# A four-layer attention kernel: gates folded into the memory's mask and into ScalarE's copy, residual sums of layer B moved from VectorE to ScalarE and GpSimd

## The chip, the cores and the metric

The kernel runs on one core of one Trainium2 chip, as one launch. The metric is device time in microseconds (us) for the whole program. TensorE (PE) does the matrix products, with its weight loads shown apart (PEld), VectorE (DVE) and ScalarE (ACT) the work on tiles, GpSimd (POOL) some of the elementwise work, and SyncE (SP), ScalarE and GpSimd issue the transfers.

## The reference

Four layers in the order A, B, A, B, each a residual sum on a layer norm; sequence S = 2048, width D = 640, H = 32 heads of 20. Layer A is linear attention, layer B causal attention within 4 segments of 512 rows plus a memory of the earlier segments. The part of B that the change touches:

```python
g = sigmoid(beta)                       # one gate per head
for s in range(4):
    logits = einsum(qs, ks) * scale + mask
    p = softmax(logits)
    a_dot = einsum(p, vs)
    pq = phi(qs)                        # phi(t) = t + 1 if t > 0 else exp(t)
    a_mem = einsum(pq, M) / (einsum(pq, z) + 1e-6)
    outs.append(g * a_mem + (1.0 - g) * a_dot)
    M = M + einsum(phi(ks), vs);  z = z + sum(phi(ks))
x = x + concat(outs) @ wo               # the residual sum
```

## The kernel before

**The streams.** PE's instructions stand in an order that the program writes (MANUAL names PE alone). Kernel.run mixes two generators by the costs that each reports: dense (projections, layer norms, memory, output projections) and attention. The order of DVE, ACT, POOL and SP, and which of the 8 banks of PSUM each product is written to, are left to the scheduler. A bank (tag "ps") is handed on when the last reader of the product in it is done, so a matrix product of one stream can wait for a reader of the other.

**Attention of layer B.** A segment has 8 groups of 4 heads, so each layer has 32 groups and the program 64. The table STRETCHES lists a group's steps in three stretches; a slot works on three groups at once: row maxima of the newest, exponentials of the one before, and the sums and the output of the oldest. In a slot:

- row_max (L687, L694): PE multiplies queries by keys into two banks, DVE takes the row maximum of each piece with a custom instruction on 128, 256, 384 or 512 columns, each followed by a short read of the accumulator into mg.
- split_max and max_rows (L703 to L718): the maxima are split into two fp16 numbers, turned by PE and copied into two spare rows of the query stack, so that a second product subtracts them.
- scores (L729, L733, L740): PE writes the shifted scores, ACT takes exponentials (pe, ten buffers), POOL zeroes what lies above the diagonal.
- weigh (L756): PE multiplies the exponentials by the values; the values carry a 21st column of ones per head, so that row 20 of a head's 32 rows is the softmax denominator.
- evacuate (L762): ACT copies the 128x512 result from PSUM to oTf.
- normalize (L769 to L782): PE turns oTf in four pieces into one bank; DVE takes the reciprocal of the denominators (L772, 128x16), multiplies it by 1 - g (L773, 128x16), and multiplies the values by it (L781, or L778 in segment 0), which is the last reader of the bank; POOL adds the product to what the memory gave (L782).

Just after the four turns PE issues the first maxima's products and the second group's first scores, so DVE's queue there holds, beside L772, L773 and L781, the two 512-wide row maxima of the newest group.

**Memory of layer B.** phi of the keys times the values is added up in acc (L587, L589). masked (L478) multiplies acc by the block mask blk, which keeps each head to its own rows. read_mem (L359) multiplies phi of the queries by that; DVE adds 1e-6 to the denominators (L377), takes the reciprocal (L378), for layer B multiplies by the gate (L380), and multiplies the values (L381). Layer B calls it for the four row tiles of each of segments 1 to 3, two halves each, 48 halves in the two layers.

**Output of layer B.** b_out turns the rows of a segment (turn, L268 to L273), multiplies them by wo in two halves of 320 columns (proj_n, 15 products each), and o_half (L391) takes each half from PSUM with one DVE instruction: times a scale, plus the rows of x. When both halves are done, ACT's queue issues the transfer of the row tile (L662). Each layer B has 16 row tiles, so 32 halves, 64 in the program. In the first layer B these lie between 560 and 1022 us, mixed with layer A; in the last one all four segments' outputs stand behind the projections, in the last 150 us, beside the last nine groups' attention.

**Queues.** Loads and q, k stores go by SP, the fetches of weights and phi of layer A's queries by POOL, the row tiles x by ACT.

## Time and profile before

| what | value |
|---|---|
| median of 3 runs | 1830.17 us (1827.09 to 1830.6) |
| profiled execution: time, span | 1833.06 us, 1831.3 us |
| mean granted TensorE clock | 0.995 |
| PE busy | 1713.7 us, 94% of the span, 13032 instructions |
| DVE busy | 1145.0 us, 63%, 3890 instructions |
| ACT busy | 911.1 us, 50%, 1696 instructions |
| POOL busy | 502.5 us, 27%, 925 instructions |
| opening, 0 to 130 us: PE busy | 111.23 us |
| 130 to 310 us, first half of layer A: PE busy | 179.75 of 180 us |
| 310 to 998 us, attention of the first layer B: PE busy | 635.99 of 688 us |
| 998 to 1220 us, second layer A: PE busy | 221.71 of 222 us |
| 1220 to 1831.3 us, attention of the last layer B: PE busy | 565.01 of 611.3 us |

Shares are of the span, the time from the first to the last instruction on the core; the profiled execution took 1.8 us more than its span. The clock is the share of full speed that TensorE was granted. A line like L694 is a line of the kernel before; the changed kernel's lines are some 13 to 15 higher from L391 on (L694 is its L708, L733 its L747, L762 its L776, L772 its L786, L781 its L793, L662 its L676, L272 its L284).

In a row of the timeline stand the start in us, the duration in us, the engine, the line, the operation, the tiles (written <- read), the shape, and in brackets how long the engine had been idle before it and what ended that. "mg" in such a bracket is the end of a row maximum: PE waited for the bank that the maximum had read.

### The profile page before, as it was taken

The numbers are of one execution on the slowest core, as the hardware profiler recorded it, in microseconds if no ns is written. First come the engines' busy times: TensorE is split into PE (matmuls) and PEld (weight loads), VectorE is DVE, ScalarE is ACT, GpSimd is POOL, SyncE is SP. The second block draws the span as 40 slices with busy tenths as digits, with TensorE's granted clock in tenths as the row PEclk, the third lists the DMA queues.
The fourth block names the chain that finished last, engine by engine and source line by source line (L and its number), as shares of the span: only waits on it lengthen the run. The fifth ranks groups of instructions, "written<-read, shape, count | busy, mean of one in ns | idle before, by whom it ended". The sixth has DMA issues, their size and how long they took to land.

```text
span 1831.3 us, 36161 instructions
## 1 busy us (share of the span) xinstructions
PE 1713.7 (94%) x13032; PEld 1070.3 (58%) x13032; DVE 1145.0 (63%) x3890; ACT 911.1 (50%) x1696; POOL 502.5 (27%) x925
## 2 busy tenths in 40 slices
PE   6999999999999999898989999999999989998998
PEld 4666676654664565453556776766546546544555
DVE  7655343677777676766663421527687777777783
ACT  5455433256556545545554433333664665565553
POOL 1534440022122113224344334200221231232231
PEclk9999999999999999999999999999999999999999
DMA  7452443312222332352212112432122222323332
GB/s 254 154 188 92 159 143 99 107 58 93 88 67 86 105 103 76 105 186 71 66 56 87 51 33 91 137 108 99 51 91 92 86 90 91 101 77 100 122 112 87
DMA packets 123307, 185.96 MB, mean 102 GB/s; under 512 B 13676, under 2 KB 85484, under 8 KB 120952
## 3 DMA queue, kind: packets, MB, share of 16 engines
q1 hardware_dynamic: 109416, 137.44, 23.5%
q0 software_dynamic: 4496, 25.23, 3.8%
q10 hardware_dynamic: 9216, 20.98, 3.0%
q8 instruction: 103, 1.69, 0.4%
q14 instruction: 76, 0.62, 0.1%
HBM read 104.41 MB, written 78.64 MB: 100 GB/s over the span
## 4 chain that ended last, share of the span: by engine, by line
PE 75%; DVE 11%; ACT 6%; issue 4%; POOL 2%; DMA 2%; SPq 1%; POOLq 0%; ACTq 0%; DVEq 0%
PE ps L325 33%; PE ps L311 18%; PE ps L756 7%; DVE junk L694 4%; PE ps L268 4%; ACT pe L733 3%; PE ps L370 3%; PE ps L729 3%; PE ps L452 2%; PE ps L687 2%; POOL e L341 1%; PE ps L582 1%; PE ps L769 1%; DVE nat L547 1%; PE ps L574 1%
## 5 line engine op out<-in xcount | busy, mean ns | idle before, releaser
L694 DVE CUSTOM_DVE_ANT_0 junk<-ps,maskw 128x512 bf16<-128x512 f32 (+3 forms) x1024 | 499.5, 488 | 83.2 <-PE ps L687 27.1
L733 ACT ACTIVATE pe<-ps,lsc 128x512 f32<-128x512 f32 x640 | 392.7, 691 | 174.5 <-PE ps L729 171.5
L740 POOL TENSOR_SCALAR_AFFINE_SELECT pe<-pe 128x256 f32<-128x256 f32 (+1 forms) x640 | 233.5, 371 | 677.4 <-ACT pe L733 672.0
L325 PEld LDWEIGHTS <-xT 128*128 128x128 f16 x2880 | 281.7, 99 | 124.1 <-issue 18.6
L325 PEld LDWEIGHTS <-oT 128*128 128x128 f16 x1920 | 187.1, 98 | 79.6 <-issue 7.6
L341 POOL TENSOR_SCALAR e<-e 128x320 f32<-128x320 f32 (+1 forms) x104 | 163.7, 1574 | 163.2 <-ACT e L337 154.4
L756 PE MATMUL ps<-pe,v 128*32 128x512 f32 (+3 forms) x2048 | 155.4, 438 | 13.7 <-ACT pe L733 6.8
L729 PE MATMUL ps<-qs,ks 62*128 62x384 f16 (+3 forms) x1024 | 132.2, 299 | 33.4 <-DVE mg L694 22.4
L325 PE MATMUL ps<-w_Bo,oT 128*128 128x320 f16 x960 | 142.8, 301 | 2.6 <-DVE mg L694 1.4
L325 PE MATMUL ps<-w_Bv,xT 128*128 128x320 f16 x960 | 141.3, 301 | 1.9 <-DVE mg L694 1.9
L325 PE MATMUL ps<-w_Av,xT 128*128 128x320 f16 x960 | 141.2, 305 | 1.6 <-DVE w_Av L234 1.0
L311 PE MATMUL ps<-xT,w_Bq 128*128 128x512 f16 x600 | 139.5, 379 | 1.5 <-DVE mg L694 0.9
L311 PE MATMUL ps<-xT,w_Bk 128*128 128x512 f16 x600 | 139.5, 379 | 0.2 <-DVE xn L391 0.2
L325 PE MATMUL ps<-w_Ao,oT 128*128 128x320 f16 x960 | 139.5, 299 | 0.0
L311 PE MATMUL ps<-xT,w_Aq 128*128 128x512 f16 x600 | 136.0, 379 | 1.3 <-DVE xT L273 0.9
L325 PE MATMUL ps<-w_Ak,xT 128*128 128x320 f16 x960 | 135.6, 299 | 1.4 <-DVE mg L694 1.4
L348 ACT ACTIVATE v<-ps 128x320 f32<-128x320 f32 x128 | 55.4, 436 | 143.2 <-PE ps L325 138.9
L291 POOL TENSOR_TENSOR rs<-rs,mhalf 128x1 f32<-128x1 f32 x64 | 35.3, 551 | 302.6 <-DVE rs L290 302.6
L687 PE MATMUL ps<-ks,qs 60*128 60x512 f16 (+3 forms) x1024 | 108.4, 297 | 5.8 <-ACT pe L733 3.6
L756 PEld LDWEIGHTS ps<-pe,v 128*32 128x32 f32 x2048 | 65.3, 110 | 81.2 <-issue 66.3
L547 DVE SCALAR_TENSOR_TENSOR nat<-ps,nat 128x512 f16<-128x512 f32 x80 | 55.3, 691 | 90.3 <-ACT nat L546 86.4
L546 ACT ACTIVATE nat<-ps 128x512 f16<-128x512 f32 x80 | 48.0, 600 | 105.9 <-PE ps L311 76.3
(151 smaller groups left out, 2240.9 us busy)
## 6 DMA issues: line engine op xcount, KB each, us to landing
x<-xn ACTq DMA_DIRECT2D x48, 320.0 KB
qs<-qd SPq DMA_DIRECT2D x128, 120.0 KB
ks<-kd SPq DMA_DIRECT2D x128, 120.0 KB
xo<-x SPq DMA_DIRECT2D x48, 320.0 KB
pqd<-pq POOLq DMA_DIRECT2D x40, 256.0 KB, 2.5
pqi<-pqd SPq DMA_DIRECT2D x32, 320.0 KB
qd<-nat SPq DMA_DIRECT2D x40, 256.0 KB
kd<-nat SPq DMA_DIRECT2D x40, 256.0 KB
```

The costliest lines, as they stand in the source:

```text
L268: nc.tensor.transpose(pt[:, (c - c0) * P:(c - c0 + 1) * P], src[:, c * P:(c + 1) * P], self.ident)
L311: nc.tensor.matmul(p, w[:, c, a, t * P:(t + 1) * P], xT[:, c, b, :], start=k == 0, stop=k == 3 * C - 1)
L325: nc.tensor.matmul(p, xT[:, c, a, i * P:(i + 1) * P], w[:, c, b, n * HN:(n + 1) * HN], start=k == 0, stop=k == 3 * C - 1)
L341: nc.gpsimd.tensor_scalar(e, e, 1.0, eps, op0=OP.min, op1=OP.add)
L348: self.nc.scalar.activation(vv[:, n * HB:(n + 1) * HB, :DH], p.rearrange("p (h e) -> p h e", e=DH), AF.Copy, scale=V_SHIFT)
L547: nc.vector.scalar_tensor_tensor(nat[:, 1], p, QK_SHIFT, nat[:, 0], op0=OP.mult, op1=OP.subtract)
L687: nc.tensor.matmul(bs[par][:, a:a + n], qs[r, p, i * P:(i + 1) * P], ks[r, p, :n], start=True, stop=True)
L694: nc.vector.tensor_tensor_reduce(junk[:, :n], bs[par][:, a:a + n], self.maskw[:, SEG - n:], 1.0, NEG, OP.add, OP.max, G["mg"][:, par, p, i ...
L729: nc.tensor.matmul(b[:, a:a + n], ks[r, p, j * P:(j + 1) * P], qs[r, p, j * P:], start=True, stop=True)
L733: nc.scalar.activation(e, b, AF.Exp, scale=self.lsc)
L740: nc.gpsimd.affine_select(d, d, pattern=pat, compare_op=OP.is_ge, fill=0.0, base=0, channel_multiplier=-1)
L756: nc.tensor.matmul(G["pv"][32 * h4:32 * h4 + 32, j * P:], v[j][:, h * E1:h * E1 + 32], G.pop((p, par, j)), start=j == 0, stop=j == 2, skip ...
```

## The change

Three edits, and a smaller ring for POOL's transfers.

1. **1 - g** moves into evacuate. A new tile cg (128 x 8) holds 1/(1 - g) in the four rows where the denominators of a group's heads lie, 1 elsewhere. It is filled once by four small transfers on SP, one exponential on ACT, and a memset and a two-step tensor_scalar on DVE. The copy of L762 multiplies by a column of it, so the denominators arrive multiplied by 1/(1 - g) and the reciprocal of L772 brings 1 - g with it. L773 is gone (64 instructions).
2. **g** moves into the mask. gblk is blk with its value columns multiplied by the gate, made once by a 128x756 copy and five tensor_tensor on DVE; masked takes it for layer B. L380 is gone (48 instructions).
3. **The residual sum** of layer B's output, for all but the last segment of the last layer B (56 of 64 halves): instead of one DVE instruction, ACT copies the half from PSUM with the scale (new L404) and POOL adds the rows of x in place (new L405). The transfer L662 (new L676), on ACT's queue, now follows POOL's add.

The ring that POOL's transfers use shrinks from 8192 to 4096 bytes.

```diff
     def gates(self):
...
+        self.cg = cp.tile([P, NG], F32, name="cg")
+        nc.vector.memset(self.cg, -1e4)
+        for h4 in range(4):
+            nc.sync.dma_start(self.cg[32 * h4 + DH:32 * h4 + DH + 1],
+                              bass.AP(tensor=beta.tensor, offset=beta.offset + h4, ap=[[0, 1], [4, NG]]))
         nc.scalar.activation(g, g, AF.Exp, scale=-1.0)
+        nc.scalar.activation(self.cg, self.cg, AF.Exp)
         nc.vector.tensor_scalar(g, g, 1.0, None, op0=OP.add)
         nc.vector.reciprocal(g, g)
-        self.gate = g
-        self.gate1 = cp.tile([P, H], F32, name="gate1")
-        nc.vector.tensor_scalar(self.gate1, g, -1.0, 1.0, op0=OP.mult, op1=OP.add)
+        nc.vector.tensor_scalar(self.cg, self.cg, 1.0, 2.0 ** 100, op0=OP.add, op1=OP.min)
+        self.gblk = cp.tile([P, MW], F32, name="gblk")
+        nc.vector.tensor_copy(self.gblk, self.blk)
+        for t in range(C):
+            n = HI[t] - LO[t] + 1
+            b = self.gblk[:, OFF[t]:OFF[t] + WID[t]].rearrange("p (h e) -> p h e", e=E1)[:, :, :DH]
+            nc.vector.tensor_tensor(b, b, g[:, LO[t]:HI[t] + 1, None].to_broadcast([P, n, DH]), op=OP.mult)
...
-    def read_mem(self, pq, mem, dst, mul=None):
+    def read_mem(self, pq, mem, dst):
...
-            if mul is not None:
-                nc.vector.tensor_tensor(rc, rc, mul[:, k * HB:(k + 1) * HB], op=OP.mult)
...
-    def o_half(self, oT, wo, L, x, xn, n):
+    def o_half(self, oT, wo, L, x, xn, n, later=False):
+        nc = self.nc
         p = self.proj_n(oT, wo, 0, n)
-        self.nc.vector.scalar_tensor_tensor(xn[:, n * HN:(n + 1) * HN], p, self.io[L],
-                                            x[:, n * HN:(n + 1) * HN], op0=OP.mult, op1=OP.add)
+        c = slice(n * HN, (n + 1) * HN)
+        if later:
+            nc.scalar.activation(xn[:, c], p, AF.Copy, scale=self.io[L])
+            nc.gpsimd.tensor_tensor(xn[:, c], xn[:, c], x[:, c], op=OP.add)
+        else:
+            nc.vector.scalar_tensor_tensor(xn[:, c], p, self.io[L], x[:, c], op0=OP.mult, op1=OP.add)
...
-                st["mem"] = self.masked(acc)
+                st["mem"] = self.masked(acc, self.gblk)
...
-                self.o_half(oT[i], wo, "B", x, xn, n)
+                self.o_half(oT[i], wo, "B", x, xn, n, later=not st.get("ends"))
...
-        self.nc.scalar.activation(G["oT"], G["pv"], AF.Copy)
+        self.nc.scalar.activation(G["oT"], G["pv"], AF.Copy, scale=self.cg[:, G["g"]:G["g"] + 1])
...
-        nc.vector.tensor_tensor(rc, rc, self.gate1[:, None, 4 * g:4 * g + 4].to_broadcast([P, NT, 4]),
-                                op=OP.mult)
...
+                segs[-1]["ends"] = True
```

PE's instructions keep their order in the whole program; 1915 of its 2372 products go to another bank than before, since the banks follow their readers. DVE, ACT and POOL are ordered anew by the scheduler. Two places show how.

The first is DVE in the group of the last layer B that is normalized at 1741 us (the fourth of the last nine). Before, the reciprocal is followed by the two 512-wide maxima with L773 between them, and only then by the product L781, which reads the bank of the turned output:

```order
3585 L273 TENSOR_TENSOR oT<-ps,oT 128x2x128
3586 L391 SCALAR_TENSOR_TENSOR xn<-ps,ioB,xo 128x320
3587 L772 RECIPROCAL rc_22429<-ps 128x16
3588 L694 ISA junk,mg<-ps,maskw 128x512
3589 L694 ISA mg 128x1
3590 L773 TENSOR_TENSOR rc_22429<-rc_22429,gate_2322 128x16
3591 L694 ISA junk,mg<-ps,maskw 128x512
3592 L694 ISA mg 128x1
3593 L781 TENSOR_TENSOR tmp<-ps,rc_22429 128x320
3594 L694 ISA junk,mg<-ps,maskw 128x384
```

The same place in the changed kernel:

```order
3443 L285 TENSOR_TENSOR oT<-ps,oT 128x2x128
3444 L786 RECIPROCAL rc_22378<-ps 128x16
3445 L708 ISA junk,mg<-ps,maskw 128x512
3446 L708 ISA mg 128x1
3447 L793 TENSOR_TENSOR tmp<-ps,rc_22378 128x320
3448 L708 ISA junk,mg<-ps,maskw 128x512
3449 L708 ISA mg 128x1
3450 L708 ISA junk,mg<-ps,maskw 128x384
```

The residual sum (L391) and L773 are gone, and the product (L781, now L793) stands between the two maxima instead of behind both. PE's third product after the two is then written to the product's bank instead of the second maximum's. The same exchange is found in most of the 64 groups: the sequence reciprocal, maximum, L773, maximum, product, with nothing else between, stands in 36 groups before; reciprocal, maximum, product in 40 after.

The second is ACT in the same group. Before, the copy of the group's result is followed by a piece of the turned rows, the transfer of the row tile, and four exponentials:

```order
1193 L762 ACTIVATE oTf<-ps 128x512
1194 L272 ACTIVATE oT<-ps 128x2x128
1195 L662 DMA out_x<-xn 128x640
1196 L733 ACTIVATE pe<-ps,lsc 128x512 x4
1197 L272 ACTIVATE oT<-ps 128x3x128
```

And after:

```order
1245 L776 ACTIVATE oTf<-ps,cg 128x512
1246 L284 ACTIVATE oT<-ps 128x2x128
1247 L404 ACTIVATE xn<-ps,ioB 128x320
1248 L676 DMA out_x<-xn 128x640
1249 L747 ACTIVATE pe<-ps,lsc 128x512 x4
1250 L284 ACTIVATE oT<-ps 128x3x128
1251 L404 ACTIVATE xn<-ps,ioB 128x320
```

The scaled copy stands ahead of the transfer, and the transfer, which reads what POOL adds to that copy, ahead of the exponentials. The copy, the transfer and exponentials stand directly behind one another like this at 5 places of the program, 4 of them in the last 150 us; at the other row tiles the transfer stands later in ACT's queue.

More of the change, by code (lines that the diff above doesn't have):

```diff
@@ L462, in memory @@
             if s == NSEG - 1:
-                L["mem"] = self.masked(acc)
+                L["mem"] = self.masked(acc, self.blk)
         if behind:
@@ L474, in a_first, with masked @@
             yield from queries(range(2, C))
-    def masked(self, acc):
+    def masked(self, acc, blk):
         mem = self.sb.tile([P, MW], F32, tag="mem", name="mem", bufs=2)
-        self.nc.vector.tensor_tensor(mem, acc, self.blk, op=OP.mult)
+        self.nc.vector.tensor_tensor(mem, acc, blk, op=OP.mult)
         return mem
@@ L626, in b_memory @@
             for i in range(NT):
-                yield from self.read_mem([q[:, i * P:(i + 1) * P] for q in st["pq"]], mem,
-                                         st["o"][:, i], self.gate)
+                yield from self.read_mem([q[:, i * P:(i + 1) * P] for q in st["pq"]], mem, st["o"][:, i])
         st["remembered"] = True
@@ L1010 @@
     arrays["const"] = constants()
-    nc = bacc.Bacc("TRN2", target_bir_lowering=False, num_devices=1, dynamic_dma_scratch_size=8192)
+    nc = bacc.Bacc("TRN2", target_bir_lowering=False, num_devices=1, dynamic_dma_scratch_size=4096)
     build(nc, arrays)
```

## The prediction

> **What bounds the kernel now.** I read the chain of waits first. By engine it says:
>
> ```profile
> PE 75%; DVE 11%; ACT 6%; issue 4%; POOL 2%; DMA 2%; SPq 1%; POOLq 0%; ACTq 0%; DVEq 0%
> ```
>
> TensorE sets the end. Nothing in the change removes work of PE, so it can only shorten PE's idle time. The second view, the windows of the two attention stretches, says how much there is (columns: length, then busy time of PE, PEld, DVE, ACT, POOL):
>
> ```profile
> 310.00:998.00 688.00, 635.99 (x5015) 380.01 (x5013) 467.39 (x1700) 363.54 (x673) 181.98 (x393) 1.00 0.28 91
> 1220.00:1831.30 611.30, 565.01 (x4586) 334.81 (x4584) 442.27 (x1629) 328.24 (x606) 142.79 (x356) 0.99 0.29 94
> ```
>
> PE is idle 688.00 - 635.99 = 52.0 us in the first and 611.30 - 565.01 = 46.3 us in the second: 98.3 us is the most that can be won. DVE is busy 909.7 us of these 1299.3 and ACT 691.8, neither full. The third view, PE's waits, says whom PE waits for (us in total, times, longest):
>
> ```profile
> PE ps L729 <- DVE mg L694: 22.4, 42, 1.0
> PE ps L268 <- DMA x<-in_A_x: 11.5, 1, 11.5
> PE ps L268 <- DVE mg L694: 7.1, 15, 0.5
> PE ps L756 <- ACT pe L733: 6.8, 17, 0.7
> PE pm L712 <- DVE m L704: 6.0, 9, 1.2
> PE ps L325 <- DVE mg L694: 5.2, 10, 1.0
> ...
> PE ps L370 <- DVE rc L377: 3.2, 4, 0.8
> ```
>
> The largest item by far is the end of a row maximum on DVE: 22.4 + 7.1 + 5.2 = 34.7 us in 67 waits, a third of the idle time. The change touches the place where these waits arise. The fourth view is DVE's timeline in one group, normalized at 1741 us:
>
> ```profile
> 1740.75 0.55 DVE L391 SCALAR_TENSOR_TENSOR xn<-ps,ioB,xo 128x320 f32<-128x320 f32 x1 [0.99 <-PE ps L325]
> 1741.22 0.25 DVE L772 RECIPROCAL rc<-ps 128x16 f32<-128x16 f32 x1
> 1741.51 0.69 DVE L694 CUSTOM_DVE_ANT_0 junk<-ps,maskw 128x512 bf16<-128x512 f32 x1
> 1742.12 0.08 DVE L694 DVE_READ_ACCUMULATOR2_ANT mg<- 128x1 f32 x1
> 1742.12 0.17 DVE L773 TENSOR_TENSOR rc<-rc,gate 128x16 f32<-128x16 f32 x1
> 1742.35 0.69 DVE L694 CUSTOM_DVE_ANT_0 junk<-ps,maskw 128x512 bf16<-128x512 f32 x1
> 1742.97 0.08 DVE L694 DVE_READ_ACCUMULATOR2_ANT mg<- 128x1 f32 x1
> 1742.97 0.48 DVE L781 TENSOR_TENSOR tmp<-ps,rc 128x320 f32<-128x320 f32 x1
> 1743.37 0.55 DVE L694 CUSTOM_DVE_ANT_0 junk<-ps,maskw 128x384 bf16<-128x384 f32 x1
> ```
>
> and PE's next step there:
>
> ```profile
> 1743.10 0.55 PE L268 MATMUL ps<-ident,ol 128*128 128x128 f32 x3 [0.47 <-DVE mg L694]
> ```
>
> The second 512-wide maximum starts at 1742.35 and takes 0.69, so it ends at 1743.04; PE starts at 1743.10, 0.06 later, in the bank that this maximum had read. It had waited 0.47.
>
> This recurs all over both stretches. I sorted PE's waits behind the two 512-wide maxima of a group into three kinds: 26 single waits of 0.47 behind the second (390.38 below is the first, 1743.10 above one of the last), ten pairs of 0.35 behind the first and 0.47 behind the second (432.10 with 432.94 is the first), and 18 single waits of 0.3 to 1.05 behind the first only, where DVE had other work ahead of it (1683.11 is the last):
>
> ```profile
> 390.38 0.44 PE L268 MATMUL ps<-ident,xh 128*128 128x128 f32 x2 [0.47 <-DVE mg L694]
> ...
> 432.10 0.37 PE L729 MATMUL ps<-qs,ks 62*128 62x512 f16 x1 [0.35 <-DVE mg L694]
> 432.94 0.37 PE L729 MATMUL ps<-qs,ks 62*128 62x512 f16 x1 [0.47 <-DVE mg L694]
> ...
> 1683.11 0.61 PE L729 MATMUL ps<-qs,ks 62*128 62x512 f16 x2 [0.58 <-DVE mg L694]
> ```
>
> **The change part by part.** Group rows below give count, busy time in all and mean ns.
>
> *L773 goes.* By itself this is worth next to nothing where it stands as at 1741 us: there 0.84 us lie between the starts of the two maxima with L773 between them. The timeline a few us earlier shows two maxima of the same size with nothing between them:
>
> ```profile
> 1735.79 0.69 DVE L694 CUSTOM_DVE_ANT_0 junk<-ps,maskw 128x512 bf16<-128x512 f32 x1
> 1736.40 0.08 DVE L694 DVE_READ_ACCUMULATOR2_ANT mg<- 128x1 f32 x1
> 1736.63 0.69 DVE L694 CUSTOM_DVE_ANT_0 junk<-ps,maskw 128x512 bf16<-128x512 f32 x1
> ```
>
> Again 0.84. L773's 0.17 fit into a gap that is there anyway. What its removal does is let the product L781 be placed where L773 stood. The order of the changed kernel has it so: maximum, product, maximum. The product then starts at 1742.12 and ends 0.48 later, at 1742.60, and since it is the last reader of the turned output, its bank is free then; the changed order gives PE's next product this bank. With the same 0.06 PE starts at 1742.66 instead of 1743.10: 0.44 earlier, and of the wait of 0.47 only 0.03 is left. The second maximum starts 0.40 after the product, the distance from 1742.97 to 1743.37 above, so at 1742.52, 0.17 later than before; the 384-wide one then 0.84 later, at 1743.36, as before. The bank of the second maximum goes to a product that PE writes two or three steps later, so the 0.17 hurts nobody.
>
> The sum: 26 singles x 0.44 = 11.4 us. In the ten pairs the first wait stays and the second goes: 10 x 0.44 = 4.4. Among the 18 others the product comes ahead of a 512-wide maximum in about ten; PE then waits for 0.48 of work instead of 0.69, which gives 10 x 0.21 = 2.1 (between 0 and 18 x 0.21 = 3.8). Together 17.9 us.
>
> *L380 goes.*
>
> ```profile
> L380 DVE TENSOR_TENSOR rc<-rc,gate 128x16 f32<-128x16 f32 x48 | 8.2, 171 | 0.3
> ```
>
> The four waits for L377 in PE's waits (3.2 us) are PE waiting for the memory's readers; each has one L380 of 0.171 in its chain: 4 x 0.17 = 0.7. The other 44 lie beside PE's work. Between 0 and 1.4; I take 0.7.
>
> *L391 goes from DVE in 56 halves.*
>
> ```profile
> L391 DVE SCALAR_TENSOR_TENSOR xn<-ps,ioB,xo 128x320 f32<-128x320 f32 x64 | 35.1, 549 | 53.1 <-PE ps L325 52.8
> ```
>
> That is 56 x 0.549 = 30.7 us, 3.4% of DVE's 909.7. Almost all follow PE directly (52.8 us of idle ahead of them end with PE), so they stand on PE's path only when a row maximum is queued behind one. Taken as 3.4% of the 34.7 us: 1.2; bounded by 0 and by one such wait of 0.47 in ten of the 56 places, 4.7. I take 1.0.
>
> So 17.9 + 0.7 + 1.0 = 19.6 us can be gained. Against it stand two engines that get this work.
>
> *ACT* gets 56 copies of 128x320 with a scale from a tile. L337 is such an instruction on the same shape, and L733 one of 128x512:
>
> ```profile
> L733 ACT ACTIVATE pe<-ps,lsc 128x512 f32<-128x512 f32 x640 | 392.7, 691 | 174.5 <-PE ps L729 171.5 <-POOL pe L740 1.8 <-PE ps L687 0.9
> ```
>
> ```profile
> L337 ACT ACTIVATE e<-ps,inv_Ak 128x320 f32<-128x320 f32 x64 | 33.7, 526 | 50.1 <-PE ps L325 49.6
> ```
>
> That makes 56 x 0.526 = 29.5 us. The copy of L762 also gets its scale from a tile; ACT's timeline has it without, beside the exponentials:
>
> ```profile
> 1738.43 0.60 ACT L762 ACTIVATE oTf<-ps 128x512 f32<-128x512 f32 x1 [1.40 <-PE ps L756]
> 1738.93 0.38 ACT L272 ACTIVATE oT<-ps 128x256 f16<-128x256 f32 x1
> 1741.33 0.34 ACTq L662 DMA_DIRECT2D out_x<-xn  x1
> 1742.00 2.42 ACT L733 ACTIVATE pe<-ps,lsc 128x512 f32<-128x512 f32 x4 [2.69 <-PE ps L729]
> ```
>
> 0.691 (L733, with a tile) against 0.60: 64 x 0.09 = 5.8 us. ACT's load in the two stretches goes from 691.8 to about 727 of 1299.3 us, 53% to 56%. The copy of L762 ends at 1739.03, the reciprocal behind the turns that read it starts at 1741.22, so the 0.09 is hidden in that gap; without that cover it would be up to 5.8 us. The transfer is the sharper point. It now waits for copy and add: L391 ended at 1740.75 + 0.55 = 1741.30, just ahead of the transfer's 1741.33; copy and add end at 1740.75 + 0.53 + 0.86 = 1742.14 (estimate, with the add's 0.86 from the row below), if the copy starts when the product is ready, as L391 did. The issue's 0.34 follows, and the exponentials behind it start at 1742.5 instead of 1742.00. PE wants the first one's bank after its three turns, at about 1742.66 + 0.39 = 1743.05, and gets it at 1742.5 + 0.69 + 0.06 = 1743.25. So here 0.2 of the 0.44 is lost again, and at worst all of it. There are five such places: 5 x 0.2 = 1, up to 5 x 0.5 = 2.5. Elsewhere the transfer stands behind later work. The other copies may stand ahead of exponentials that PE waits for (6.8 us in 17 waits before); 56 copies, a sixth of them in the way by half their length, 56 / 6 x 0.26 = 2.4; I take 1 of it, since all 640 exponentials together made PE wait only 17 times. And a PE that comes 0.44 earlier meets ACT sooner: a sixth of the 17.9, 3.0, is my guess, between 0 and half, 9. ACT's cost: 1 + 1 + 3.0 = 5 us, between 0 and 2.5 + 2.4 + 9.
>
> *POOL* gets 56 adds of 128x320. L782 is the same operation on the same shape:
>
> ```profile
> L782 POOL TENSOR_TENSOR otok<-otok,tmp 128x320 f32<-128x320 f32 x48 | 41.4, 863 | 85.6 <-DVE tmp L781 85.4
> ```
>
> So 56 x 0.863 = 48.3 us on 324.8 busy in the two stretches, 25% to 29%. POOL also zeroes the upper triangles of the exponentials; these have ten buffers and are summed a slot later, so that an add ahead of one is mostly hidden. If one add in four stood ahead of a mask that PE waits for at once, 14 x 0.86 = 12; at the other end nothing. The exposed waits of PE for POOL's masks do not appear among the large ones above, so I take 2, near the low end.
>
> The exchange as a whole: the add alone takes POOL 0.863 where DVE did scale, add and eviction in 0.549. The Trainium skill, GPSIMD Engine Reference, section Engine selection, speaks against this edit: it puts an elementwise add on VectorE and calls GpSimd about twice as slow for two inputs. By the rule the edit costs and brings nothing, since it gives up the 1.0 and adds the costs of ACT's copies and POOL (2 + 2); the kernel without it would gain 19.6 - 1.0 - 3.0 = 15.6. By the rows it is a loss as well, of about 3, only hidden by the rest.
>
> *The setup* (cg, gblk) lies in the opening and the first layer A:
>
> ```profile
> 130.00:310.00 180.00, 179.75 (x1202) 123.51 (x1201) 78.55 (x177) 72.98 (x137) 65.90 (x56) 1.00 0.37 131
> ```
>
> DVE is less than half busy there, 78.55 of 180 us, behind a full PE; the smaller ring holds fewer descriptors, but no wait for it is among PE's. Both at 0, up to 1 us each.
>
> Sum: 19.6 - 5 - 2 = 12.6, rounded to 12 for the setup. Against the profiled execution, 1833.06 - 12 = 1821; the median of the runs shown, 1830.17, is 2.9 lower, so the forecast is 1818.
>
> **The rivals.**
> *More of it is kept.* Nothing is lost to ACT and POOL: 19.6 us, and the DVE relief at its upper 4.7 makes it 23.3: 1807 to 1811. For it speaks that ACT is only 53% busy and PE's waits for it are short; against it the 0.2 worked out above.
> *PE meets ACT instead.* Half of the 17.9 returns as waits for exponentials (L756, L325 <- ACT), and the other costs stay: 17.9/2 + 1.7 - 4 = 6.6, so 1823 to 1826. For it speaks that ACT's exponentials are the next thing that PE needs; against it that at 1742 they start from PE's own scores, which come 0.44 earlier too if the two scores are ahead of them.
> *It does not do what it says.* L773 and L380 lie in gaps, so removing them frees no time on DVE, and the banks follow the measured ends in another way than I read. Then only 1.7 of gain stands against 4 of cost: about 1830 to 1833.
> *Slower: the transfer blocks ACT.* Each of the 28 row tiles' transfers waits on ACT's queue for POOL's add, and POOL has masks queued ahead of it, so an add ends 0.8 to 1.7 after the copy; all exponentials behind it start late, and the row maxima's banks no longer decide. At 28 x 1.0 = 28 us against 19.6 the kernel is 8 us slower: 1838. It turns at 19.6 / 28 = 0.7 us per transfer. For it speak the order at 5 places; against it that at the other 23 the transfer comes later in ACT's order, when the add should be done.
>
> **How the numbers follow.** About 0.2% (3.7 us) is what a measurement of this kernel can tell from no change. Forecast (1813 to 1823): 0.45. More kept (1804 to 1812): 0.17. PE meets ACT (1823 to 1826): 0.17. Doing nothing (1827 to 1833): 0.10. Slower (1834 to 1842): 0.11. Faster is 0.45 + 0.17 + 0.17 = 0.79, same 0.10, slower 0.11. Leaving out the slower case and the outer third of the case that keeps more, the range is 1806 to 1831.
>
> **What the profile after would show.** Right: the waits of L729, L268 and L325 for mg fall from 34.7 us to about 17, those of L377's chain from 3.2 to about 2.5; PE's idle time in the two stretches falls from 98.3 to about 86; in a group the product stands between the maxima, and PE's step behind it comes without the 0.47. ACT's waiting for xn's add would show as idle time ahead of L676 and of exponentials behind it, at the 5 places, by some 0.5 us. Wrong: if the mg waits stay, the reading of the banks is wrong; if they go but PE's idle time stays, ACT or POOL stands in PE's waits in their place, L756 and L325 above all; if the L676 rows show long idle times, the slower case is there.

## The result, and the profile after

| | before | changed |
|---|---|---|
| median | 1830.38 us (4 runs, 1827.09 to 1831.97) | 1818.7 us (4 runs, 1815.73 to 1820.7) |
| ratio | 1 | 0.9926, 95% interval 0.9913 to 0.994 |
| profiled execution: time, span | 1833.06 us, 1831.3 us | 1820.7 us, 1818.9 us |
| PE busy | 1713.7 us | 1716.8 us |
| PE idle (span less busy) | 117.6 us | 102.1 us |
| mean granted clock | 0.995 | 0.994 |

The span is 12.4 us shorter: PE is idle 15.5 us less and, with the same instructions in the same order, busy 3.1 us more. The chain that ended last is PE's as before:

```profile
PE 75%; DVE 11%; ACT 5%; issue 4%; POOL 2%; DMA 2%; SPq 1%; ACTq 0%; POOLq 0%; DVEq 0%
```

Because the order of PE is unchanged, its instructions can be laid side by side: nearly all of the 13032 match. The stretch that began at 310 and ended at 998 us now runs from 311.45 to 989.57, the one from 1220 on now from 1211.56. These are their windows (length, then busy time of PE, PEld, DVE, ACT, POOL):

```profile
311.45:989.57 678.12, 635.27 (x5015) 378.21 (x5013) 450.68 (x1617) 377.99 (x700) 204.27 (x420) 1.00 0.28 92
1211.56:1818.90 607.34, 567.89 (x4586) 334.72 (x4584) 427.40 (x1549) 340.67 (x630) 162.34 (x380) 0.99 0.29 94
```

PE is idle 42.9 us in the first (before: 52.0) and 39.4 in the second (46.3). DVE lost 31.6 us of work, ACT took 26.9 and POOL 41.8 more. PE's waits, in the changed kernel's line numbers:

```profile
PE ps L743 <- DVE mg L708: 12.1, 23, 0.9
...
PE ps L382 <- DMA pqi<-pqd: 3.3, 2, 2.5
...
PE ps L770 <- POOL pe L754: 2.8, 4, 1.6
...
PE pm L726 <- DVE nat L562: 1.3, 1, 1.3
...
PE ps L337 <- DVE mg L708: 0.5, 1, 0.5
```

The three rows behind the row maxima, 22.4 + 7.1 + 5.2 = 34.7 us before, are now 12.1 + 0.5 = 12.6; the row of L268 (now L280) for mg is gone. What grew are the small rows between: the transfer pqi (1.5 us before), POOL's masks (1.2) and nat, the tile of a q or k projection on its way to a store (no such row before).

The group that was normalized at 1741 us is now at 1729 us. DVE's timeline there:

```profile
1729.00 0.69 DVE L708 CUSTOM_DVE_ANT_0 junk<-ps,maskw 128x512 bf16<-128x512 f32 x1
1729.62 0.08 DVE L708 DVE_READ_ACCUMULATOR2_ANT mg<- 128x1 f32 x1
1729.62 0.49 DVE L793 TENSOR_TENSOR tmp<-ps,rc 128x320 f32<-128x320 f32 x1
1730.02 0.68 DVE L708 CUSTOM_DVE_ANT_0 junk<-ps,maskw 128x512 bf16<-128x512 f32 x1
1730.63 0.08 DVE L708 DVE_READ_ACCUMULATOR2_ANT mg<- 128x1 f32 x1
1730.86 0.56 DVE L708 CUSTOM_DVE_ANT_0 junk<-ps,maskw 128x384 bf16<-128x384 f32 x1
```

and PE's:

```profile
1729.02 1.10 PE L743 MATMUL ps<-qs,ks 62*128 62x512 f16 x4
1730.21 0.52 PE L280 MATMUL ps<-ident,ol 128*128 128x128 f32 x3
1730.93 1.25 PE L337 MATMUL ps<-w_Bo,oT 128*128 128x320 f16 x8 [0.20 <-ACT pe L747]
```

The product stands between the two maxima, starts with the end of the first, and is done at 1729.62 + 0.49 = 1730.11; PE's turns follow at 1730.21 with no wait listed (the gap is 0.08, it was 0.47). The third maximum starts 1.86 after the first, as it did before. And PE then waits 0.20 for the first exponential's bank. ACT's rows there show why:

```profile
1728.25 0.53 ACT L404 ACTIVATE xn<-ps,ioB 128x320 f32<-128x320 f32 x1 [1.34 <-PE ps L337]
1729.75 0.34 ACTq L676 DMA_DIRECT2D out_x<-xn  x1
1730.19 2.42 ACT L747 ACTIVATE pe<-ps,lsc 128x512 f32<-128x512 f32 x4 [1.41 <-PE ps L743]
```

POOL's row for the add:

```profile
1728.86 0.86 POOL L405 TENSOR_TENSOR xn<-xn,xo 128x320 f32<-128x320 f32 x1 [3.84 <-ACT xn L404]
```

The copy ends at 1728.78, the add at 1729.72, the transfer is issued at 1729.75, and the exponentials start at 1730.19. That is 1.19 after the start of the first maximum (1729.00); before it was 0.49 (1741.51 and 1742.00), so they come 0.7 later against the rest of the group.

### The profile page after: what moved, and what is told of

It reads as the page before. It is cut to its first block, busy times and chain, and to the rows that moved or that the text cites. A ratio compares the mean times of both kernels' runs of the same rounds, so it can differ in the third digit from the quotient of the medians.

```text
span 1818.9 us, 36252 instructions
## 1 busy us (share of the span) xinstructions
PE 1716.8 (94%) x13032; PEld 1068.9 (59%) x13032; DVE 1112.6 (61%) x3729; ACT 940.2 (52%) x1753; POOL 549.1 (30%) x981
## 4 chain that ended last, share of the span: by engine, by line
PE 75%; DVE 11%; ACT 5%; issue 4%; POOL 2%; DMA 2%; SPq 1%; ACTq 0%; POOLq 0%; DVEq 0%
PE ps L337 32%; PE ps L323 18%; PE ps L770 7%; DVE junk L708 4%; PE ps L743 3%; PE ps L280 3%; PE ps L382 3%; ACT pe L747 2%; PE ps L701 2%; PE ps L467 2%; PE ps L597 1%; POOL e L353 1%; PE ps L783 1%; DVE st L298 1%; DMA qs<-mt 1%
## 5 line engine op out<-in xcount | busy, mean ns | idle before, releaser
L337 PEld LDWEIGHTS <-xT 128*128 128x128 f16 x2880 | 281.5, 99 | 123.1 <-issue 9.2
L337 PEld LDWEIGHTS <-oT 128*128 128x128 f16 x1920 | 186.9, 98 | 80.3 <-issue 6.0
L770 PE MATMUL ps<-pe,v 128*32 128x512 f32 (+3 forms) x2048 | 155.9, 439 | 13.1 <-ACT pe L747 5.9
L743 PE MATMUL ps<-qs,ks 62*128 62x512 f16 (+3 forms) x1024 | 132.4, 299 | 24.1 <-DVE mg L708 12.1
L337 PE MATMUL ps<-w_Bo,oT 128*128 128x320 f16 x960 | 142.2, 301 | 2.9 <-ACT oT L284 1.2
L337 PE MATMUL ps<-w_Av,xT 128*128 128x320 f16 x960 | 142.0, 306 | 1.1 <-DVE w_Av L246 1.0
L337 PE MATMUL ps<-w_Bv,xT 128*128 128x320 f16 x960 | 141.6, 301 | 0.1
L337 PE MATMUL ps<-w_Ao,oT 128*128 128x320 f16 x960 | 139.5, 299 | 0.0
L337 PE MATMUL ps<-w_Ak,xT 128*128 128x320 f16 x960 | 135.6, 299 | 0.6 <-DVE tmp L793 0.6
L770 PEld LDWEIGHTS ps<-pe,v 128*32 128x32 f32 x2048 | 64.8, 110 | 82.7 <-issue 67.4
L323 PEld LDWEIGHTS <-w_Bq 128*128 128x128 f16 x600 | 57.2, 99 | 71.2 <-issue 9.7
```

What stands on the lines that cost most here:

```text
L323: nc.tensor.matmul(p, w[:, c, a, t * P:(t + 1) * P], xT[:, c, b, :], start=k == 0, stop=k == 3 * C - 1)
L337: nc.tensor.matmul(p, xT[:, c, a, i * P:(i + 1) * P], w[:, c, b, n * HN:(n + 1) * HN], start=k == 0, stop=k == 3 * C - 1)
L743: nc.tensor.matmul(b[:, a:a + n], ks[r, p, j * P:(j + 1) * P], qs[r, p, j * P:], start=True, stop=True)
L770: nc.tensor.matmul(G["pv"][32 * h4:32 * h4 + 32, j * P:], v[j][:, h * E1:h * E1 + 32], G.pop((p, par, j)), start=j == 0, stop=j == 2, skip ...
```

## The experiments

All are timed against the kernel before on the same chip. The table gives the ratio and, from each profile, where PE's time went: busy time, idle time ahead of PE's instructions from 130 us on (without the some 4 us that follow PE's last instruction), and of that idle time what ended with a row maximum, with other work of DVE, with ACT, POOL and a transfer, in us; the rest is gaps of 0.15 us and less.

| kernel | ratio, 95% interval | PE busy | idle | row max | other DVE | ACT | POOL | transfer |
|---|---|---|---|---|---|---|---|---|
| before | 1 | 1713.7 | 94.8 | 36.3 | 22.9 | 18.7 | 6.3 | 3.0 |
| changed | 0.9926 (0.9913 to 0.994) | 1716.8 | 79.1 | 12.6 | 22.3 | 20.0 | 7.7 | 6.0 |
| e1 gates only | 0.9902 (0.9886 to 0.9918) | 1712.1 | 76.6 | 14.2 | 23.6 | 18.2 | 6.6 | 3.6 |
| e2 sums only | 1.0023 (1.001 to 1.0036) | 1711.7 | 99.6 | 38.0 | 24.3 | 21.0 | 5.4 | 3.8 |
| e3 step in the chain | 1.0025 (1.0016 to 1.0035) | 1714.8 | 97.6 | 37.3 | 24.2 | 20.4 | 5.4 | 3.4 |
| e4 step beside | 0.9951 (0.9933 to 0.9969) | 1718.4 | 82.9 | 15.6 | 26.1 | 19.5 | 7.8 | 3.2 |
| e5 rows by SP | 0.9992 (0.9971 to 1.0014) | 1715.8 | 87.3 | 12.9 | 31.9 | 17.5 | 7.7 | 6.9 |
| e6 first gate | 0.9924 (0.9907 to 0.994) | 1710.8 | 79.3 | 14.7 | 24.1 | 18.6 | 6.0 | 5.5 |
| e7 sums, last layer | 0.9919 (0.9906 to 0.9932) | 1719.6 | 76.2 | 13.3 | 23.1 | 19.5 | 6.0 | 4.0 |
| e8 sums, first layer | 0.993 (0.9917 to 0.9944) | 1715.8 | 78.2 | 13.1 | 22.6 | 22.2 | 4.5 | 5.1 |
| e9 gates, three nat | 0.9897 (0.9882 to 0.9913) | 1715.9 | 77.9 | 15.0 | 23.3 | 18.0 | 6.6 | 4.3 |
| e10 three nat | 0.9923 (0.991 to 0.9936) | 1715.8 | 77.8 | 12.6 | 21.4 | 19.8 | 7.7 | 6.2 |
| e11 changed again | 0.9922 (0.9909 to 0.9935) | 1716.5 | 81.0 | 12.6 | 26.7 | 19.6 | 7.7 | 4.0 |
| e12 gates again | 0.9909 (0.9896 to 0.9922) | 1714.6 | 75.9 | 12.4 | 23.6 | 18.4 | 6.0 | 4.8 |

PE's busy time differs by up to 9 us between profiles of the same PE instructions, and by 2.5 between e1 and e12, which are the same kernel. It goes with the granted clock: 1710.8 and 1712.1 us in the two profiles at 0.997 (e6, e1), 1719.6 in the one at 0.992 (e7). The time of one kernel does the same: the six runs of e6 took 1813.82 to 1815.07 us at 0.996 and 0.997 and 1819.4 to 1821.62 at 0.994. The idle time is therefore the better measure of one profile, and a difference of 2 or 3 us between medians has to be read beside the clocks.

**e1, the gates without the exchange of the sums.** The edit to the changed kernel:

```diff
-                self.o_half(oT[i], wo, "B", x, xn, n, later=not st.get("ends"))
+                self.o_half(oT[i], wo, "B", x, xn, n, later=False)
```

> The two gate edits alone; layer B's residual sums stay with VectorE (L391 as before). Theory (order and banks): the gain is made by the product moving ahead of the second maximum, which this kernel keeps, and the exchange of the sums is a small loss. By the terms of the prediction 17.9 + 0.7 - 3.0 = 15.6 us under before, so about 1815, some 3 us under the changed kernel. Rival (the exchange helps): VectorE's 30.7 us of sums were in PE's way, four of PE's waits for xn (0.3 to 1.1 us in the trace before) are gone in the changed kernel, and without the exchange the time is 1821 to 1824.

Measured: 1814.25 us median, ratio 0.9902, which is 17.9 us of 1830 where the theory had 15.6; the rival's 1821 to 1824 lies outside the interval. Without the exchange the kernel is no slower, so the exchange is not where the gain comes from.

**e2, the exchange alone.** The kernel before, with the changed o_half and its call:

```diff
-                self.o_half(oT[i], wo, "B", x, xn, n)
+                self.o_half(oT[i], wo, "B", x, xn, n, later=not st.get("ends"))
```

> The exchange of the residual sums alone; both gate multiplications stay on VectorE as before. Theory: VectorE keeps the order maximum, gate, maximum, product, PE keeps its waits of 0.47, and the exchange costs 1.0 - 2 - 2 = -3: about 1833, between 1829 and 1836. Rival (VectorE's load is what counts): 30.7 us less of VectorE work out of 909.7 is more than the 19.4 us of the gates, and should give most of the gain: 1822 or less.

Measured: 1.0023, with an interval above 1, some 4 us slower than before, where the theory had 3. PE's waits (L734 is L729 of the kernel before, L699 its L694):

```profile
PE ps L734 <- DVE mg L699: 23.9, 44, 1.2
...
PE pm L717 <- DVE nat L552: 4.8, 1, 4.8
```

The waits for maxima are all there (22.4 before), although DVE has 24 us less to do in this profile (1120.9 against 1145.0). DVE's load is not what made them. The 4.8 us for nat was not expected; it is as much as PE's idle time grew (94.8 to 99.6), and is taken up under e10.

**e3 and e4, the same DVE step in two places.** Both add to the changed kernel one multiplication of the 16 reciprocals by a tile of ones per group; it changes no value. In e3 the product needs it, in e4 it goes to a tile that nothing reads:

```diff
 # e3, behind nc.vector.reciprocal(rc, ...)
+        nc.vector.tensor_tensor(rc, rc, self.unit[:, None, 4 * g:4 * g + 4].to_broadcast([P, NT, 4]),
+                                op=OP.mult)
 # e4, behind nc.gpsimd.tensor_tensor(o, o, tmp, op=OP.add)
+        idle = sb.tile([P, NT, 4], F32, tag="idle4", name="idle4", bufs=2)
+        nc.vector.tensor_tensor(idle, rc, self.unit[:, None, 4 * g:4 * g + 4].to_broadcast([P, NT, 4]),
+                                op=OP.mult)
```

> The changed kernel with one more VectorE step per group: the reciprocals are multiplied by a tile of ones, 128x16, between L772's successor and the product, so VectorE has the order maximum, step, maximum, product again; the gates stay where the change put them. Theory: the waits of 0.47 come back in some 36 groups, 36 x 0.44 + 2.1 = 17.9 less what PE had lost of it to ScalarE (3): 15 us above the changed kernel, about 1833. Rival (VectorE's load): 64 x 0.17 = 11 us of 940 more work; PE's remaining waits for VectorE grow by about 1%, under 1 us: 1819 to 1820.

> The changed kernel with the same 128x16 multiplication by ones, but written to a tile that nothing reads and placed behind the product: VectorE does the same work as in the kernel with the step in the chain, and keeps the order maximum, product, maximum. Theory: PE's bank comes free as early as in the changed kernel, the second maximum is 0.17 to 0.2 later, which few wait for: 1819 to 1822. Rival (VectorE's load or each step behind the reciprocal costs its time): the same as with the step in the chain.

Measured: e3 1.0025, e4 0.9951. DVE's busy time is 1119.5 us in the one and 1120.6 in the other. DVE's timeline of e3 in the group shown above:

```profile
1744.48 0.69 DVE L710 CUSTOM_DVE_ANT_0 junk<-ps,maskw 128x512 bf16<-128x512 f32 x1
1745.10 0.08 DVE L710 DVE_READ_ACCUMULATOR2_ANT mg<- 128x1 f32 x1
1745.10 0.17 DVE L789 TENSOR_TENSOR rc<-rc,unit 128x16 f32<-128x16 f32 x1
1745.33 0.69 DVE L710 CUSTOM_DVE_ANT_0 junk<-ps,maskw 128x512 bf16<-128x512 f32 x1
1745.94 0.08 DVE L710 DVE_READ_ACCUMULATOR2_ANT mg<- 128x1 f32 x1
1745.94 0.48 DVE L797 TENSOR_TENSOR tmp<-ps,rc 128x320 f32<-128x320 f32 x1
```

with PE's

```profile
1746.08 0.55 PE L282 MATMUL ps<-ident,ol 128*128 128x128 f32 x3 [0.47 <-DVE mg L710]
```

and DVE's timeline of e4:

```profile
1734.81 0.69 DVE L710 CUSTOM_DVE_ANT_0 junk<-ps,maskw 128x512 bf16<-128x512 f32 x1
1735.43 0.08 DVE L710 DVE_READ_ACCUMULATOR2_ANT mg<- 128x1 f32 x1
1735.43 0.49 DVE L795 TENSOR_TENSOR tmp<-ps,rc 128x320 f32<-128x320 f32 x1
1735.83 0.17 DVE L798 TENSOR_TENSOR idle<-rc,unit 128x16 f32<-128x16 f32 x1
1735.91 0.68 DVE L710 CUSTOM_DVE_ANT_0 junk<-ps,maskw 128x512 bf16<-128x512 f32 x1
```

In e3 the wait of 0.47 is back to the hundredth, and all of the gain is gone; in e4 the product leads and PE's turns come without a listed wait. So it is the place of the product in DVE's queue that counts, not the 11 us of DVE work. e4's 0.9951 of 1830.17 is 1821, within the expected 1819 to 1822. Its profile, like that of e3, has the wait of 4.8 us for nat that e2 has, against 1.3 in the changed kernel, and a few waits of 0.4 to 0.65 for a maximum that its step made late:

```profile
657.82 0.96 PE L384 MATMUL ps<-mem,pq 128*128 128x147 f32 x6 [0.45 <-DVE mg L710]
```

**e6, the first edit alone.** The gates kernel with blk and L380 as before, and only cg left:

```diff
-                st["mem"] = self.masked(acc, self.gblk)
+                st["mem"] = self.masked(acc, self.blk)
...
             nc.vector.reciprocal(rc, rc)
+            if mul is not None:
+                nc.vector.tensor_tensor(rc, rc, mul[:, k * HB:(k + 1) * HB], op=OP.mult)
```

> Of the three edits only the first: 1 - g in ScalarE's copy, so that L773 goes; the gate of the memory (L380) and the residual sums stay on VectorE. Theory: this edit alone makes the order maximum, product, maximum and carries all but 0.7 us of the gain: 1815 to 1816, ratio to the kernel before 0.990 to 0.992, and the four waits for L377 stay at 0.8 us each. Rival (both gates weigh by their time on VectorE, 11.2 and 8.2 us): it gives 58% of the gain of both gates, ratio about 0.9943.

Measured: 1817.24 us, 0.9924. The ratio is a little over the 0.990 to 0.992 that was written down; the rival's 0.9943 lies outside the interval, by little. The row maxima's waits are down from 36.3 to 14.7, as far as in e1. The waits for the memory's readers are as before,

```profile
PE ps L377 <- DVE rc L384: 3.2, 4, 0.8
```

and 2.4 us in e1 and in the changed kernel. The first edit carries the gain. The medians of e6 and e1 are 3 us apart, but the runs of e6 had clocks of 0.994 to 0.997 and those of e1 of 0.995 to 0.997; the two profiled executions, both at 0.997, have spans of 1812.1 and 1812.3 us. So nothing speaks against the 0.8 us of this row as what the second edit is worth.

**e5, the transfer on SP's queue.** The changed kernel with

```diff
-            self.q_x.dma_start(dst[r:r + P], xn)
+            nc.sync.dma_start(dst[r:r + P], xn)
```

in b_out.

> The changed kernel with layer B's row tiles sent by SP's queue instead of ACT's, so that ACT never waits for GpSimd's add. Theory: the five places at which exponentials stand behind the transfer get their 0.3 to 0.4 us back, 1.5 us in all, so 1817 and PE's waits of L337 for ACT go away; the rest of what the exchange costs stays. Rival 1 (the transfer on ACT's queue is what costs the 4 us between the changed kernel and the one with the gates alone): 1814 to 1815. Rival 2 (the wait only moves to SP): loads of query and key stacks stand behind the transfer on SP and come late: 1822 or more, with waits of L701 or L743 for qs<-qd.

Measured: 0.9992; nearly all of the gain is lost, and the second rival was right that it gets slower, though by another row than it named. In the profile PE's idle time grew by 8.2 us (79.1 to 87.3) of the 12 that the ratio lost. The rest is not explained by a wait: the granted clock of these runs was 0.988 to 0.994 (0.962 in one), that of the kernel before on this chip 0.993 to 0.998, and why it was lower stays open. The waits of ACT fell from 20.0 to 17.5 us, as the theory said. PE's two waits that are new or longer are

```profile
1727.72 0.52 PE L280 MATMUL ps<-ident,ol 128*128 128x128 f32 x3 [3.87 <-DMA ol<-od]
```

and, in the first layer,

```profile
812.07 0.27 PE L726 MATMUL pm<-ident,m 128*32 128x128 f16 x1 [10.20 <-DVE nat L562]
```

The first is the wait moved to SP: the load of a spilled row tile, issued at 1724.32, stood behind a transfer that waited for POOL's add and was issued at 1723.92. The second is 1.3 us in the changed kernel; the last section comes back to it.

**e7 and e8, the exchange in one layer.** The changed kernel with the exchange in the last layer B (24 halves) or the first (32):

```diff
-                ... later=not st.get("ends"))
+                ... later=dst is self.out and not st.get("ends"))    # e7
+                ... later=dst is not self.out)                       # e8
```

> The changed kernel with the exchange of the residual sums in the last layer B only (24 halves, in the last 150 us); the first layer B keeps its 32 on VectorE. Theory: in the last stretch the exchange takes four waits for ACT of 0.3 to 0.4 us and gives back four waits for xn of 0.3 to 0.5 us, so it is worth nothing there, and the time is that of the gates alone, ratio 0.990 to 0.991. Rival (the transfers queued behind GpSimd's add in the last stretch are what the exchange costs): ratio 0.9926, that of the changed kernel.

> The changed kernel with the exchange in the first layer B only (32 halves, between 560 and 1022 us); the last layer keeps its sums on VectorE. Theory: the loss lies here, where an xh, a nat copy or a mask is set behind the new copy or the add (a wait of 1.3 us for nat at 805 us and of 1.6 us for a mask at 850 us in the changed kernel's trace, up to 4.8 us at the first place in the other kernels with the exchange): ratio 0.992 to 0.9935. Rival (the loss lies in the last stretch): ratio 0.990.

Measured: e7 0.9919, between its two expectations; e8 0.993, within the theory's 0.992 to 0.9935. The idle times agree, e7 76.2 us, e1 76.6, e8 78.2, but the intervals overlap, and the ratios do not settle which layer carries the loss. The rows say where the waits arise: e8's profile has PE's wait for nat (1.2 us) and that of 1.6 us for a mask, e7's has neither.

**e9 and e10, a third buffer for nat.** nat is the tile between ACT's copy of a q or k projection and its store. The gates kernel and the changed kernel with

```diff
-        nat = self.bp.tile([P, 2, SEG], F16, tag="nat", name="nat", bufs=2)
+        nat = self.bp.tile([P, 2, SEG], F16, tag="nat", name="nat", bufs=3)
```

> The gates alone (residual sums on VectorE) with three buffers for nat, the tile between ACT's copy of a projection and its store, instead of two. Theory: with the sums on VectorE PE waits 0.01 us for nat at the place (805 us) where the kernels with the exchange wait 1.3 to 4.8 us, so a third buffer changes nothing: ratio 0.989 to 0.992, PE idle after the opening as with two buffers, 76 to 78 us. Rival (nat holds up ACT all along in the two attention stretches): 2 us or more under that.

> The changed kernel with three buffers for nat instead of two. Theory: in the kernels with the exchange ACT's next copy to nat waits for the landing of an earlier store, which meets the fetch of a weight; the third buffer takes that wait away, PE's wait of L726 for nat goes from 1.3 to 0, and PE's idle time after the opening falls from 79.1 by about 1 us: ratio 0.991 to 0.992. Rival 1 (the store's landing is also what PE's next step needs, as kd is read back for the key stack): the wait only moves to qs<-mt or to ks, no gain, ratio 0.9926. Rival 2 (the exchange costs through POOL and ACT, not through nat): the same, no gain.

Measured: e9 0.9897, e10 0.9923. The wait of 1.3 us for nat at 805 us is gone in e10, but the wait of L743 for qs<-mt that follows it is 0.8 longer:

```profile
PE ps L743 <- DMA qs<-mt: 3.8, 2, 2.1
```

(2.7 us in the changed kernel). So the theory and its first rival were each half right: PE's idle time fell by 1.3 us, and the ratio did not move. In e9 nothing changed, as expected. With three buffers PE's idle time is the same with the exchange (77.8) and without it (77.9).

**e11 and e12, the changed kernel and the gates alone, side by side.** No edits.

> The changed kernel, unaltered, beside the kernel with the gates alone on the same chip, since their ratios (0.9926 and 0.9902) have intervals that overlap by a little. Theory (the exchange is a small loss): ratio 0.9915 to 0.994, above that of the gates alone by 0.001 to 0.003. Rival (no difference; the gap is chance): the two ratios within 0.0005 of each other.

> The gates alone, unaltered, beside the changed kernel on the same chip. Theory: ratio 0.989 to 0.9915, under the changed kernel's by 0.001 to 0.003, which is 2 to 5 us; of these 2 are PE's idle time (100.3 us against 102.1 in the profiles). Rival: within 0.0005 of the changed kernel's.

Measured: 0.9922 and 0.9909, 0.0013 apart. Three pairs now show the same sign: 0.9926 and 0.9902 (each against its own runs of before), 0.9923 and 0.9897 (with three buffers), 0.9922 and 0.9909; and e2 against before, +0.0023. No single pair of intervals is clear of the other, e2's is clear of 1. By the ratios the exchange costs 0.0013 to 0.0026, 2 to 5 us.

The profiles say more about where this arises. In e11, which is the changed kernel unaltered, PE's wait for nat was 5.1 us, where the first profile of the same kernel has 1.3:

```profile
808.30 0.60 ACT L561 ACTIVATE nat<-ps 128x512 f16<-128x512 f32 x1 [5.70 <-DMA kd<-nat]
```

That copy came 4 us later than the changed kernel's (804.14). Set beside the idle time that the exchange adds, the wait for nat makes up half of it or all of it: 2.5 us more idle time in the changed kernel than in e1, with 1.3 for nat; 5.1 in e11 over e12, with 5.1; 4.8 in e2 over before, with 4.8; and none in e10 over e9, where a third buffer takes the wait away. What is left between e10 and e9 goes with the clock: e9's runs had 0.995 to 0.997, e10's 0.994 and 0.995, and whether the kernel has a part in that stays open. So with two buffers the gates alone have the lower ratio and less idle time in both pairs and are the better version, by little; that they are so with three is not shown.

## Why the prediction was right

The time (1818, measured 1818.7) and the cause were right. Some terms were off, and that their errors balanced so closely was luck.

**L773, 17.9 us.** Matched one by one, the 37 waits of 0.47 that the profile before has (36 were counted) fell from 17.5 to 3.4 us: 14.1, against 15.8 expected. Where PE goes on with turns (L268) 0.08 to 0.12 stays instead of 0.03; elsewhere it is the 0.03. The waits of 0.35 behind the first maximum stayed, as said, 4.2 and now 4.7. The other 21 fell from 14.6 to 9.8, which is 4.8, against 2.1 expected. In eleven of them a product now stands ahead of the first maximum; that is about the ten counted on, but each gave 0.28 to 0.38 instead of 0.21. In seven the order of maxima and product is as before and only L773, which stood ahead of the first maximum, is gone, 0.09 each. At some places the bank that PE waits for is now the product's, so that the row in the list changed its name (L743 for otok and tmp, L337 for tmp, 2.8 us). Together 14.1 - 0.5 + 4.8 = 18.4. e3 gives all of it back with one step in the chain, e4 does not: the mechanism is shown. That the multiplication itself costs next to nothing is borne out by those seven places, 0.6 us together, and by e4, whose extra step of the same size, behind the product, costs a few places only.

**L380, 0.7 us.** The four waits fell from 3.2 to 2.4. Right.

**L391, 1.0 us of relief.** PE's waits for xn from DVE (1.7, 0.8 and two of 0.2 us) are gone from the changed kernel, so the relief is 2.9, within the bounds and above the value taken. They stand in e1, which is no slower all the same. The longest of them, 1.1 us at 854 us, comes back 3.6 us later as the wait of 1.6 for a mask that is told under POOL.

**ACT, 5 us.** In three parts. The transfer ahead of the exponentials was priced at 0.2 us per place; the row at 1730.93 shows 0.20, and PE's waits of L337 for exponentials are four with 0.8 us in all. Of the copies ahead of exponentials, taken at 1, the rows show two waits of L770 for a copy itself, 0.6 us. The 3.0 us for "a PE that comes earlier meets ACT sooner" was a guess, and it failed: in e1, where PE comes as early, the waits for ACT are 18.2 us against 18.7 before. The whole of ACT's waits rose by 1.3 us in the changed kernel.

**POOL, 2 us.** The waits that end with POOL rose by 1.4. One place carries them, 1.6 us at 850 us: a weighted sum waits for masks, which stand behind a store of POOL's and an add of 0.87. That is the rival's mechanism at one place of 56.

**What the sum left out.** One cost of the exchange is in no term. A layer norm's ACT instruction (L310) stands ahead of a copy to nat at 798 us, in e1 as in the changed kernel; with the exchange it came some 0.5 us later against PE, and the store of that copy then left just behind a weight fetch instead of just ahead of it (below). PE's wait for nat there is 1.3 us in the changed kernel, 4.8 in e2, e3 and e4 and 5.1 in e11, and e10 shows that it hangs on nat's buffers. The waits for transfers, 3.0 us before and 6.0 in the changed kernel, are 3.6 to 5.5 in the kernels without the exchange (e1, e6, e9, e12), so they are not shown to be a cost of it.

**The setup, 0.** PE's idle time in the first 130 us is 19.3 us against 18.8 (130 - 110.74, 130 - 111.23): 0.5, within the bounds. The smaller ring was not timed alone. e3, which has it, and e2, which has not, are 1.0025 and 1.0023, and nothing in them points at it.

**The sum.** The terms that gain came to 18.4 + 0.8 + 2.9 = 22.1 us where 19.6 was forecast, and what stood against them to 6.4 instead of 7, of which ACT and POOL are only 2.7; most of the rest is nat and the transfers, which differ from profile to profile. So PE's idle time after the opening fell by 15.7 us (94.8 to 79.1) where 12.6 was forecast; 3.1 us of that went to a longer busy time of PE, at a clock of 0.994 against 0.995. That time differs as much between profiles of one kernel, so the agreement of the median with the forecast to 0.7 us is better than the working deserved.

**The rivals.** That the multiplications lie in gaps and nothing changes fails by e1 (its 1.7 us of gain still count the 0.7 of L380, which it holds to be worth nothing). That the transfer blocks ACT fails by size: 0.2 us at four places, not 0.7 at 28. That PE meets ACT instead fails too: the waits that end with ACT rose by 1.3 us, not by half of the 17.9. That more is kept did not come either: even the gates alone, with 16.7 to 17.9 us (e12, e1), stay under its 19.6. The rule from the Trainium skill's GPSIMD Engine Reference, section Engine selection, that an elementwise add belongs on VectorE, agrees with this case as far as the ratios tell: the add took

```profile
L405 POOL TENSOR_TENSOR xn<-xn,xo 128x320 f32<-128x320 f32 x56 | 48.7, 869 | 113.0 <-ACT xn L404 112.7
...
L404 ACT ACTIVATE xn<-ps,ioB 128x320 f32<-128x320 f32 x56 | 29.7, 530 | 48.3 <-PE ps L337 47.9
```

0.869 on POOL on top of 0.530 on ACT, for 0.549 on DVE, and in each of the three pairs the ratio is lower without it. But of the idle time that PE lost to it half or more is the wait for nat, and not the length of the add. The sum by that rule was 15.6 us under before; e1 and e12 measured 0.0098 and 0.0091 of 1830, 17.9 and 16.7 us.

## What to carry to other kernels

Where PE waits for a bank, look at what the engine that frees it has queued ahead of the last reader, and in which order: a 0.17 us step that cost next to no time of its own kept a 0.48 us reader behind a 0.69 us one, 37 times, and was worth 0.8% of the kernel. Test such a cause by putting the same work back once in the chain and once beside it. And when an edit of many parts comes out faster, time the parts, and read the idle time and the clock beside each time: here one of three edits worked against the other two, in part by a wait that it set off elsewhere.

## What the runs showed of the hardware that was not expected

A store beside a fetch of 1600 KB on another queue can take more than twice as long to give its buffer free as one just ahead of the fetch. SP's queue in e5, where POOL's fetch of w_Av was issued at 797.48 and that of w_Ak at 800.72:

```profile
797.80 0.32 SPq L569 DMA_DIRECT2D kd<-nat  x1
798.53 0.32 SPq L568 DMA_DIRECT2D kd<-nat  x1
```

and ACT's next copy, which needs the buffer that these stores read:

```profile
810.69 0.60 ACT L561 ACTIVATE nat<-ps 128x512 f16<-128x512 f32 x1 [10.30 <-DMA kd<-nat]
```

Both stores were issued within 1.1 us behind the first fetch, and the copy came 12.2 us after the second of them, 0.3 after the second fetch had landed (810.40). In e4 the second store is issued at 799.88, 0.30 behind the fetch of w_Av (799.58), and the copy

```profile
807.42 0.60 ACT L563 ACTIVATE nat<-ps 128x512 f16<-128x512 f32 x1 [5.43 <-DMA kd<-nat]
```

comes 7.5 us after it and 0.3 after that fetch has landed (807.14). In e1 the store is issued at 799.13, 0.28 ahead of the fetch (799.41), and the copy comes 3.3 us after it, when PE has its product ready:

```profile
802.43 0.60 ACT L561 ACTIVATE nat<-ps 128x512 f16<-128x512 f32 x1 [0.62 <-PE ps L323]
```

The changed kernel lies between: its store is 0.29 behind the fetch (800.14 and 799.85), the copy comes 4.0 us after it, well ahead of the fetch's landing (807.82). In e11, the same kernel with the same 0.29 (800.49 and 800.20), the copy comes 7.8 us after the store, 0.3 after the landing (808.02); in e2 and e3 too it comes 0.3 after the fetch of w_Av has landed (812.86 and 810.21). In e12 the store is 0.04 behind the fetch, and the copy comes 3.0 us after it, when PE has its product ready. So the order of issue alone does not decide it, and one kernel can fall either way. That the fetch is the cause is read from these times; it was not tried by moving the fetch, and stays open.
